# Products of a zero tile on TensorE before the first transpositions, the first block's q products and the first projection

## The chip, the cores and the metric

The kernel runs on one core of a Trainium2 chip. The metric is the device time in microseconds (us). Three runs of the kernel before took 623.01, 628.4 and 629.44 us, so the median is 628.4 us.

## The reference

An attention layer with a memory term feeds a gated feed-forward layer.

```
scores = q @ k.T / 8, causal;  a = softmax(scores);  local = a @ v
q_p    = elu(q) + 1
mem    = (q_p @ M_prev) / (q_p @ z_prev + 1e-6)
x      = sigmoid(beta) * mem + (1 - sigmoid(beta)) * local     # 4 x 8 heads x 576 rows x 64
x      = x / rms(x) * rms_g                                    # 2304 x 512
out    = (silu(x @ w_gate) * (x @ w_val)) @ w_out              # 512 -> 1536 -> 512
```

The weights of the second layer come as 64-bit floats and are converted on the chip.

## The kernel before

The 2304 rows are 18 blocks of 128 rows, and two blocks make a chunk of 256 rows for the feed-forward layer. Blocks 0 and 1 are the first 128 rows of two batches. They, and two more, are computed in 32-bit floats; the others with pairs of 16-bit floats.

The start goes like this. `prep_qk32` (line 549) transposes k and q of a block on TensorE, four 128x128 tiles each, through `transposed` (line 528). The result stands in a PSUM tile of the tag `gv`, which has two buffers, and ScalarE or VectorE copies it out (lines 533 and 535). `prep_phi32` (line 557) does the same with elu(q)+1. `over_partitions` (line 255) finds a maximum over the partitions with two small products (lines 258 and 261). `u_scores` multiplies q by k (line 597), VectorE adds the mask and takes the row maximum (line 614), ScalarE takes the exponentials (line 666), TensorE transposes them (line 531) and `pv32` multiplies by v (line 811). `mem32` makes the memory term (lines 788 and 792). VectorE scales the local part (line 827), GpSimd adds it to the memory part (line 829). `x_norm` (line 898) squares and sums a block on ScalarE (line 391) and takes the root on GpSimd (line 904). `x_float` (line 908) then makes a diagonal matrix of the factor on VectorE (line 915), multiplies by it on TensorE (line 918), and VectorE writes the transposed block (line 919).

When blocks 0 and 1 are there, `m_proj` (line 1092) starts the projections of chunk 0 (line 1102, 32-bit) into a `gv` tile, and `m_act` takes them on ScalarE (line 1126) and VectorE (lines 1127 and 1130). From chunk 1 on the projections are 16-bit products (line 1109). `f64_to_f32` (line 1011) converts the 64-bit weights with two instructions on ScalarE (lines 1016 and 1020) and one on VectorE (line 1026), for each piece of 128 x 512; the pieces w0 to w23 come by DMA from SyncE's queue (line 978).

The order of the work on each engine is written out by hand in `ISSUE` (line 72): a letter for each kind of instruction, a number for how many of them, and `~n` for the one that stands n places further on in that kind. `T` is a transposition, `Z` one of the two small products, `S` a score product, `u` the memory term, `h` a product with v, `R` a product with the diagonal matrix, `G` a projection. Every engine works through its string in order, and `keep` (line 184) gives the instructions of a function their letter. TensorE's string begins `T8ZZ~1T8ZT4`, and around the first norm it has `s2R8G4G4~4`.

`mask` (line 291) is a 128 x 512 tile in 16-bit floats: VectorE sets it to zero (line 292), and GpSimd writes a triangle into its last 128 columns (line 293).

Of the kernel before, what the change touches and what calls it, by code (L numbers as in the profile page):

```python
# [70 lines left out]

ISSUE = {
    "PE": (
        "T8ZZ~1T8ZT4SS~1S~2S~3Zu4T4S5S~1S~2S~3T4S4u2Tu2Th4T4u4~4T2hTh3T2u4Th8ss~3ss~2ss~1s2R8G4G4~4GG~3GZG~2G3Z~1GZT4ZT4"
        "s4T4s4S8G6u4G2u4G8s~4ss~3ss~2sT4s~1s~5s2s~3ss~2ss~1s2~5s4s~1s2T4G6g9ZT4g20Zg3G2h4G5ZG2sGs~3ss~2sT4s~1ss3~1sZs3~1"
        "ss~1ss~3ss~2ss~1ss~1s4s4~4T4u4G8g6h4s8g22ZSS~1S~2S~3g16~4Zg4S4TG8u4T3Zg16DD~1D~2h4Z2D2T4DG6ZG2Dh4G8D2G8D9G32D4S"
        "S~7G16S14G3M9GMGMGMGMGM3G8S8G10S8G6D2SG24S7ZG24S5P12S3ZP12G22S16G14M8G4P12G8P12G12DD~2G11D2SD2GS~5DD~2D4G13DMP3M"
        "PSMPSS~3MPSS~2MPSS~1MPS2MPSMP15D6D~2G14D3S6DG9DD~2G5SGSGSGSGSGSGD2P24D3D~2GS6D4G13DD~2M8D4G4SGDD~2SGSGSGSGSG8D4"
        "G3MDD~2GMGMGMGMGMGD4GMGP25MPGPG3SGSGSGS3DD~2S3D4P9S3DD~2S4G24D4S4~2G6SGSG5P9G12S2D6G2P9G3SGSGSGSGSGSG14D6G5MGMGM"
        "GMGMP18GMGMGMG5SGSGSGSGSGSG2D6G5SGSGSGSGSGSP9G7SPGSPGSPGSPGSPGSPGPGP2D6G5MGMGMGMGMGMGMGMGP8GPG3SGSGSGSGSGSG2D6G5"  # L80
        "SGSGSGSGSGSG7P9G7D3SDSDSDGSGSGSP9GSGSG12SGSGSGSGSGSGSGSD6G5SGSGSGSGSP18GSGSGSG12D4MDMDMGMGMGP9MGMGMG12SGSGSGSGSG"
        "SGSGSD6G2P5GPGPGPSGPSGPSGPSGPSGSGSGSG5SGPSGPSGPSGPSGPSGPSGPSP5D6G9PGMPGMPGMPGMPGMPGMPGMPGMPGPGPGPGSGSGSGS5D6G9SG"
        "SGP10SGPSGPSGSGSGSG8D6GSGSP12GSGSGSGSGSGSG13SGP12SGSGS5D6G5SGSGSGSGSGSP12GSGSG12P12D6G5MGMGMGMGMGMGMGMG5SGSGSGSG"
        "SGSGSGSD6G5SGSP9GPSGPSGPSGSGSGSG5PGPGPGPGPGPGPGP5D3SDSDSDSGSGSGSGSGPGMPGMPGMPGMPGMPGMPGMPGMPGPGPGPGSGSGSGSGSGSGS"
        "GSD3PDPDPDGPGPGPGPGPSGPSGPSGPSGPSGSGSGSG5PGPGPGPGPGPGPGP5D4SDSDSGSGSGSGSGSPGSPGSPGSPGSPGSPGSPGSPGSPGPGPGPG3S2G5"
        "D3PDPDPDGPGPGS16PGPGPGPGPGPGPG8PGPGPGPGPGPGPS2GP4YPD4MDMDMGMGMGMGMGMS16GMGMGMGMGMGMGMGMG11D6G2S2G9S8G13D6S6PSPS"
        "P5S2P26GPGPGPGPGPGPGPGPGPGPGPGP2S8GPGPGPGPGPGPGPS8GPGPGPGPGP2S2PD6GPGPGPGPGPGPGPGPS16GPGPGPGPGPGPGPGPGPGPGPGPGP"
        "S2GPGPGP2S8P5~5PP~4PP~3PP~2DPP~1S8P~1PDPDPDPDPDPGPGPGS2PGPGPGPGPGPGPGPGPGPGPGPGPG6SGSGSGS5DSDSDS2DSDSDSM16S2GS"
        "G23D3S8D3G2P20P~10PP~9PP~8PP~7PP~6PP~5PP~4PP~3PP~2PP~1P11GPGPGPSGPSGPSGPSGPSGPSGPSGPSG5PGPGPGPGPGPGPGP5DPDPDPDPD"
        "PDPGPGPGPGPGPSGPSGPSGPSGPSGPSGPSGPSG5PGPGPGPGPGPGPGP5DPDPDPDPDPDPGPGPGPGPGPGPGPGPGPGPGPGPG5SGSGSGSGSGSGSGSD6G12"  # L90
        "M8G5MGMGMGMGMGMGMGMD6G9P24G15D5P12DG4SS~5G13PGPGPGPGPGPGPGP5D6G21S10G3D6G14S6M8S6G10D3MDMDMDMGMGMGMGMGS12G19D5P9"
        "S6DGP9G8SGSGSGSGSGSG8SGSGS6D6G13P9G6S2P9S6G5D6G14P18G3MGMGMGMGMYGMGMGMD3GS8D3G4S2P9S6G12SGSGSGSGSGSGSP9GSD6G17SG"
        "SGSGSGSGSGSGSD6S8G12M6P24M2G9P12G3D6G5SGSGSGSGSGSP12GSGSG12D6P12G24D6G13P12G11P12D6G17S2S2~6G7D4S12D2G2P12G7M8G3"
        "S16G12D6GM4GMGMSGMGMS3G14S4~2GS4G4D6P12D2D2~1S2P12S4D2S6G34MGMGMGMGMGMGMGMP12G7D6G6P12G18D3SDSDSDSGSGSP9G3PGPGPG"
        "PGPGPGPGPGPG4SGSGSGSGSGSG2D4MDMDM6P5G10PGPGPGPG4SGSGSGSGSGSG2D4PDPDPGPGPGPGPGPGPG11SGSGSGSGSGSG2D4PDPDPGPGPGPGPG"
        "PSGPSGSGSGSGSGSGSG5PGPGPGPGPGPGPGP2D4SDSDSGSGSGSGSGSPGPGPGPGPGPGPGPGPG11D3SDSDSDGSGSGSGSGSPGPGPGPGPGPGPGPGPG11D4"
        "MDMDMGMGMGMGMGMG12SGSGSGSGSGSGSGSD6G10P12G7SGSGSGSGSGSGSGSD3PDPDPDPGPGPGPGPGPGPGPGPGSGSGSGSGSGSGSGSG5MGMGMGM5D6G"
        "PGPGPGPGPGPGPGPGPGSPGSPGSPGSGSGSGSGSG4PGPGPGP5DPDPDPDPD2G9SGSGSGSGSGSGSGSG5PGPGPGP5DPDPDP2D2SDS2GSGSGSGSGSPGPGSP"
        "GSPGSPGSPGSPGSPGSPGSPGPGPG3S2G5D4PDPDPGPGPGPGS16PGPGPGPGPGPG8PGPGPGPGPGPGPS2GP3S8P2D6G5MGMGMS10GMGMGMGMGMG11M8G"
        "S11DSDSDSDSDSDG10P8S2P5GPGPGPGPGPGPGPP~10GPP~9GPP~8GPP~7GPP~6GPS8P~5GPS8P~4GPP~3PP~2PP~1P3DPDPDPDPDPDPGPGPGS2PGP"  # L100
        "GS8PGP~7PGP~6PGP~5PGP~4PGP~3PGS8P~2PGP~1PGPGPGPS2GPGPGPGPGP2GPGPGPGP3S8P2DPDPDPP~3S8PDP~2PDP~1PDPGPGPS2GPGPGPGPG"
        "PGPGPGPGPGPGPGPGPGPGS11PSGPSGPSGPSGPSGPGPGP3D6G4S2G20D2M16D4G24D6P15P7~15PP~14PP~13PP~12PP~11PP~10PP~9PP~8PP~7"
        "P15~22P15~37P52G24D6G24D8D2~1D2G48D6G24D6G24D6G24D6G24D6G24D6G24D6G24D6G24D6G24D6G24D8D2~1D4D2~1D2"
    ),
    "Activation": (
        "IfT2ITfT2IU2E4TU2E12N2fU9tU5tU4AU2ATU2oToTfE4AE4U2ATU2TU6AU4ATU4x2AU2xU2xU2E4xU2cU2xNU2AE4cxXU2U2~2cU2xAU2xU~1Ux"
# [1434 lines left out]
```

## Time and profile before

| | |
|---|---|
| median of three runs | 628.4 us |
| profiled execution | 622.36 us, with a span of 620.6 us |
| TensorE busy | 598.5 us, 96% of the span |
| weight loads on TensorE | 474.6 us, 76% |
| VectorE busy | 451.1 us, 73% |
| ScalarE busy | 396.8 us, 64% |
| GpSimd busy | 136.6 us, 22% |
| DMA | 87.57 MB |

The span goes from the first to the last instruction. PE is TensorE, DVE VectorE, ACT ScalarE, POOL GpSimd, SP SyncE. Busy time of PE is the union of its matmuls, and a matmul that runs at half the clock is busy for longer, so a busy PE may still be a slow one. [...]

### The profile page before, as it was taken

What the parts mean: (1) busy time and instruction counts of PE and PEld (TensorE: products, weight loads), DVE (VectorE), ACT (ScalarE), POOL (GpSimd) and SP (SyncE); (2) the same over time, 40 slices, a digit from 0 to 9 for tenths busy, and PEclk for the clock granted to TensorE, in tenths of its full rate; (3) what the DMA queues carried; (4) which work ended last, traced back from release to release, by engine and by line L of the source; (5) the groups of instructions that cost most, each with busy time, mean ns of one, the idle gap of its engine ahead of it and who ended that gap; (6) DMA issues with size and microseconds to landing.
All of it is one profiled execution on the core that took longest, in us unless ns stands there. A gap on an engine that the chain in (4) does not pass through costs nothing. (4 is left out here: it accounts for less than half of the span.)

```text
span 620.6 us, 15845 instructions
## 1 busy us (share of the span) xinstructions
PE 598.5 (96%) x6092; PEld 474.6 (76%) x6092; DVE 451.1 (73%) x1319; ACT 396.8 (64%) x856; POOL 136.6 (22%) x221
## 2 busy tenths in 40 slices
PE   5979999999999999999999999999999999999996
PEld 4868887677876878788888778778787888887774
DVE  3767688999999687776997777797886757853221
ACT  4587677999887667676466766875775644433221
POOL 2240001124323222121213221132221221112111
PEclk9989999999999999999999999999999999999999
DMA  7997336479868796887489379559995543520001
GB/s 264 361 335 295 103 124 202 135 172 229 149 107 164 149 178 116 176 162 125 71 146 167 80 154 188 106 109 161 164 158 108 86 91 72 94 54 18 35 1 35
DMA packets 183787, 87.57 MB, mean 141 GB/s; under 512 B 165792, under 2 KB 165792, under 8 KB 183712
## 3 DMA queue, kind: packets, MB, share of 16 engines
q1 hardware_dynamic: 180640, 81.82, 62.0%
q10 hardware_dynamic: 3072, 4.74, 2.3%
q8 instruction: 48, 0.79, 0.5%
q14 instruction: 27, 0.22, 0.1%
HBM read 37.77 MB, written 4.72 MB: 68 GB/s over the span
## 5 line engine op out<-in xcount | busy, mean ns | idle before, releaser
L1109 PE MATMUL gv<-xT,wgv 128*128 128x256 f16 x2304 | 312.6, 273 | 0.7 <-DMA xT<-x 0.5
L1109 PEld LDWEIGHTS <-wgv 128*128 128x128 f16 x2304 | 220.0, 98 | 38.9 <-issue 1.5
L1148 POOL TENSOR_TENSOR h<-th,h 128x256 f16<-128x256 f32 x88 | 65.8, 748 | 291.1 <-ACT h L1147 283.8
L674 ACT ACTIVATE S<-S,nm 128x256 f32<-128x256 f32 (+3 forms) x112 | 70.8, 639 | 41.0 <-DVE nm L614 28.4
L1127 DVE SCALAR_TENSOR_TENSOR th<-th,gv 128x256 f32<-128x256 f32 x96 | 39.9, 415 | 62.0 <-ACT th L1126 61.7
L608 PE MATMUL sc<-kT,qT 128*128 128x128 f16 x576 | 79.3, 220 | 0.8 <-DVE nm L614 0.5
L693 DVE SCALAR_TENSOR_TENSOR P<-S,P 128x512 f16<-128x512 f32 (+2 forms) x96 | 67.4, 703 | 17.4 <-ACT P L190 16.8
L1126 ACT ACTIVATE th<-gv,wt 128x256 f32<-128x256 f32 x96 | 44.5, 463 | 54.3 <-PE gv L1109 50.1
L614 DVE CUSTOM_DVE_ANT_0 S<-sc,mask,qsc 128x256 f32<-128x256 f32 (+2 forms) x96 | 57.4, 610 | 17.2 <-PE sc L608 16.7
L1184 PE MATMUL out<-wo,h 128*128 128x512 f16 x176 | 66.8, 380 | 0.0
L1183 PE MATMUL out<-wo,h 128*128 128x512 f16 x176 | 66.3, 379 | 0.0
L1185 PE MATMUL out<-wo,h 128*128 128x512 f16 x176 | 66.1, 379 | 0.0
L190 ACT ACTIVATE P<-S 128x512 f16<-128x512 f32 (+2 forms) x96 | 58.0, 605 | 12.7 <-DMA PT<-P 10.7
L1147 ACT CAST h<-th 128x256 f16<-128x256 f32 x88 | 35.1, 399 | 46.5 <-DVE th L1130 39.0
L608 PEld LDWEIGHTS <-qT 128*128 128x128 f16 x576 | 48.3, 98 | 7.3 <-issue 1.8
L1102 PE MATMUL gv<-xT,wgv 128*128 128x256 f32 x192 | 46.9, 395 | 0.8 <-DVE xT L919 0.8
L1130 DVE SCALAR_TENSOR_TENSOR th<-th,wt,gv 128x256 f32<-128x256 f32 x96 | 45.8, 477 | 1.8
L1102 PEld LDWEIGHTS gv<-xT,wgv 128*128 128x128 f32 x192 | 36.6, 197 | 7.7 <-issue 1.9
L731 PE MATMUL loc<-v,PT 128*128 128x65 f16 x288 | 40.9, 193 | 1.0 <-DMA PT<-P 1.0
L733 PE MATMUL loc<-v,PT 128*128 128x65 f16 x288 | 41.2, 193 | 0.0
L732 PE MATMUL loc<-v,PT 128*128 128x64 f16 x288 | 40.6, 194 | 0.0
L1185 PEld LDWEIGHTS <-h 128*128 128x128 f16 x176 | 17.1, 98 | 19.5
(231 smaller groups left out, 1133.5 us busy)
## 6 DMA issues: line engine op xcount, KB each, us to landing
kv<-in_qkv_dram SPq DMA_DIRECT2D x40, 256.0 KB, 3.6
q<-in_qkv_dram SPq DMA_DIRECT2D x18, 256.0 KB, 3.5
wo<-in_moe_w_out_dram SPq DMA_DIRECT2D x8, 512.0 KB, 3.9
out_dram<-res ACTq DMA_DIRECT2D x16, 256.0 KB, 3.2
wgv<-in_moe_w_val_dram SPq DMA_DIRECT2D x7, 512.0 KB, 7.7
wo<-in_moe_w_gate_dram SPq DMA_DIRECT2D x7, 512.0 KB, 9.1
qT<-qT SPq DMA_DIRECT2D x28, 128.0 KB, 3.5
wgv<-in_moe_w_gate_dram SPq DMA_DIRECT2D x5, 512.0 KB, 6.2
```

The source lines that it names most:

```text
L190: got = fn(*p, **k)
L608: nc.tensor.matmul(t[:, g * w + j * P : g * w + (j + 1) * P], qT[n][:, t2, h, :], kT[blk_of[(b, j)]][:, h, :], start=(t2 == 0), stop=(t2 = ...
L614: nc.vector.tensor_tensor_reduce(out=s[:, g * w : (g + 1) * w], in0=t[:, g * w : (g + 1) * w], in1=mask[:, m0 : m0 + w], scale=qsc[n][:, 5 ...
L674: nc.scalar.activation(v_, v_, AF.Exp, bias=nm[:, g : g + 1], scale=-1.0)
L693: m = nc.vector.scalar_tensor_tensor(out=p16[:, w : 2 * w], in0=s[:, :w], scalar=PSCALE, in1=p16[:, :w], op0=ALU.mult, op1=ALU.subtract)
L1102: nc.tensor.matmul(o, wgv[:, 1 + p, o0 : o0 + P], xT[0][:, cc, :], start=(cc == 0), stop=(cc == NC - 1))
L1109: nc.tensor.matmul(o, lhs, xT[c][:, rhs, :], start=(cnt == 0), stop=(cnt == 3 * NC - 1))
L1130: nc.vector.scalar_tensor_tensor(out=th, in0=th, scalar=sc_h, in1=gvp[F][:, 1, :], op0=ALU.mult, op1=ALU.mult)
L1148: nc.gpsimd.tensor_tensor(h16[:, 1], th, h16[:, 0], ALU.subtract)
L1183: nc.tensor.matmul(o, hh, whi, start=(f == 0), stop=False)
L1184: nc.tensor.matmul(o, hh, wlo, start=False, stop=False)
L1185: nc.tensor.matmul(o, hl, whi, start=False, stop=(f == NF - 1))
```

## The change

A new helper, `idle`, multiplies a zero tile (the first 128 columns of `mask`) by another (the next 256 columns). The product goes to a tile that the next real product overwrites. It is called in three places, and the new letter `*` puts the products in TensorE's string: 20 ahead of the first transposition, 8 ahead of the transposition of block 0's elu(q)+1, and 25 for the first projection's tile, of which 20 stand between the four `R` of block 0 and the four of block 1, and 5 between these and the first projection. Nothing else moves: without the new letters all strings are the same.

```diff
-        "T8ZZ~1T8ZT4SS~1S~2S~3Zu4T4S5S~1S~2S~3T4S4u2Tu2Th4T4u4~4T2hTh3T2u4Th8ss~3ss~2ss~1s2R8G4G4~4GG~3GZG~2G3Z~1GZT4ZT4"
+        "*20T8*8ZZ~1T8ZT4SS~1S~2S~3Zu4T4S5S~1S~2S~3T4S4u2Tu2Th4T4u4~4T2hTh3T2u4Th8ss~3ss~2ss~1s2R4*20R4*5G4G4~4GG~3GZG~2"
+    @keep("*")
+    def idle(t, count):
+        for _ in range(count):
+            nc.tensor.matmul(t, mask[:, :P], mask[:, P : 3 * P], start=True, stop=True)
+
     @keep("T")
-    def transposed(dst, src, on_act):
+    def transposed(dst, src, on_act, wait=0):
         t = ps.tile([P, NC, P], F32, tag="gv", name="tp")
+        idle(t[:, :2], wait)
...
-        transposed(k32[n], src32(n, 0), T32[0] == "a")
+        transposed(k32[n], src32(n, 0), T32[0] == "a", 20 if n == 0 else 0)
...
-        transposed(q32[n][:, 1], qst.pop(n), T32[2] == "a")
+        transposed(q32[n][:, 1], qst.pop(n), T32[2] == "a", 8 if n == 0 else 0)
...
         if m == 0:
             gvp[F] = ps.tile([P, 2, 2 * P], F32, tag="gv", name=f"gv{F}")
+            if F == 0:
+                idle(gvp[F][:, 0], 25)
```

## Rows read from the trace of the kernel before

**Rows 1.** The page: granted TensorE clock in 40 slices of 15.5 us, tenths

```profile
PEclk9989999999999999999999999999999999999999
```

**Rows 2.** Busy time by stretch: PE, PEld, DVE, ACT, POOL, granted clock, DMA

```profile
9.00:21.00 12.00, 11.98 (x55) 10.13 (x56) 4.42 (x26) 6.96 (x18) 2.28 (x5) 1.00 0.98 375
21.00:29.00 8.00, 8.00 (x72) 7.54 (x71) 7.38 (x44) 4.74 (x25) 1.45 (x2) 1.00 1.04 351
60.00:620.00 560.00, 551.04 (x5807) 434.13 (x5805) 415.12 (x1172) 357.54 (x750) 122.77 (x187) 1.00 0.62 122
```

**Rows 3.** TensorE in order, 6 to 29 us: start, duration, [idle before, releaser]

```profile
6.18 1.09 PE L531 MATMUL tp<-ident,kv 128*128 128x128 f32 x4 [6.18 <-DMA kv<-in_qkv_dram]
...
9.02 0.59 PE L258 MATMUL allp<-ident,zq 128*1 128x128 f32 x2 [0.89 <-ACT junk L391]
...
15.93 2.08 PE L788 MATMUL mem<-Mpair,q 128*128 128x128 f32 x8
...
21.24 0.66 PE L531 MATMUL tp<-ident,S 128*128 128x128 f32 x4
...
27.56 1.06 PE L788 MATMUL mem<-Mpair,q 128*128 128x128 f32 x8
```

**Rows 4.** Busy time by stretch around the first norm, columns as in Rows 2

```profile
30.80:34.20 3.40, 2.04 (x22) 1.84 (x21) 1.85 (x4) 1.47 (x4) 1.82 (x4) 1.00 1.02 355
34.20:37.60 3.40, 1.16 (x8) 0.97 (x8) 3.12 (x7) 3.40 (x7) 3.16 (x5) 1.00 0.69 233
37.60:41.00 3.40, 3.37 (x8) 2.75 (x9) 2.01 (x3) 3.40 (x8) 1.59 (x3) 0.50 0.98 309
```

**Rows 5.** TensorE in order, 31 to 84 us

```profile
31.73 1.11 PE L918 MATMUL xtp<-diag,t 128*128 128x128 f32 x8
35.69 1.16 PE L918 MATMUL xtp<-diag,t 128*128 128x128 f32 x8 [2.85 <-DVE ph L515]
37.63 6.68 PE L1102 MATMUL gv<-xT,wgv 128*128 128x256 f32 x22 [0.78 <-DVE xT L919]
...
79.73 3.62 PE L1102 MATMUL gv<-xT,wgv 128*128 128x256 f32 x16
```

**Rows 6.** Chain of waits: start, duration, 16-bit products of 128x256 in a row

```profile
609.19 2.62 PE gv L1109 x24
```

**Rows 7.** VectorE and GpSimd in order, 1 to 3 us

```profile
1.06 0.27 DVE L292 MEMSET mask<- 128x256 uint32 x1
...
2.21 0.29 POOL L293 TENSOR_SCALAR_AFFINE_SELECT mask<-mask 128x128 bf16<-128x128 bf16 x1
```

**Rows 8.** ScalarE in order, 7 to 47 us

```profile
7.31 0.58 ACT L533 COPY k<-tp 128x512 f32<-128x512 f32 x1 [1.35 <-PE tp L531]
...
8.64 0.23 ACT L391 ACTIVATE junk<-zz 128x32 bf16<-128x32 f32 x1
...
14.40 0.65 ACT L1016 ACTIVATE wgv<-wgv 128x512 f32<-128x512 f32 x1
...
15.87 0.40 ACT L666 ACTIVATE S<-S,nm 128x128 f32<-128x128 f32 x1 [0.25 <-DVE nm L614]
...
19.38 0.67 ACT L1016 ACTIVATE wgv<-wgv 128x512 f32<-128x512 f32 x1
...
21.14 0.40 ACT L666 ACTIVATE S<-S,nm 128x128 f32<-128x128 f32 x1 [0.54 <-DVE nm L614]
...
46.15 0.38 ACT L1126 ACTIVATE h32e<-gv 128x256 f32<-128x256 f32 x1 [0.85 <-PE gv L1102]
```

**Rows 9.** VectorE in order, 15 to 32 us

```profile
15.53 0.29 DVE L614 CUSTOM_DVE_ANT_0 S<-sc,mask 128x128 f32<-128x128 f32 x1 [0.89 <-PE sc L597]
...
20.81 0.29 DVE L614 CUSTOM_DVE_ANT_0 S<-sc,mask 128x128 f32<-128x128 f32 x1 [3.38 <-PE sc L597]
...
31.47 0.42 DVE L827 TENSOR_TENSOR t<-loc,den 128x256 f32<-128x256 f32 x1
```

**Rows 10.** DMA issues between 8.5 and 9.0 us: KB, us from issue to landing

```profile
wgv<-in_moe_w_gate_dram SPq DMA_DIRECT2D x1, 512.0 KB, 4.8
```

More of the change, by code (lines that the diff above doesn't have):

```diff
@@ L73 @@
     "PE": (
-        "T8ZZ~1T8ZT4SS~1S~2S~3Zu4T4S5S~1S~2S~3T4S4u2Tu2Th4T4u4~4T2hTh3T2u4Th8ss~3ss~2ss~1s2R8G4G4~4GG~3GZG~2G3Z~1GZT4ZT4"
-        "s4T4s4S8G6u4G2u4G8s~4ss~3ss~2sT4s~1s~5s2s~3ss~2ss~1s2~5s4s~1s2T4G6g9ZT4g20Zg3G2h4G5ZG2sGs~3ss~2sT4s~1ss3~1sZs3~1"
-        "ss~1ss~3ss~2ss~1ss~1s4s4~4T4u4G8g6h4s8g22ZSS~1S~2S~3g16~4Zg4S4TG8u4T3Zg16DD~1D~2h4Z2D2T4DG6ZG2Dh4G8D2G8D9G32D4S"
-        "S~7G16S14G3M9GMGMGMGMGM3G8S8G10S8G6D2SG24S7ZG24S5P12S3ZP12G22S16G14M8G4P12G8P12G12DD~2G11D2SD2GS~5DD~2D4G13DMP3M"
@@ L78 @@
[L78 to L102, printed above, removed]
@@ L103 @@
-        "P15~22P15~37P52G24D6G24D8D2~1D2G48D6G24D6G24D6G24D6G24D6G24D6G24D6G24D6G24D6G24D6G24D8D2~1D4D2~1D2"
+        "*20T8*8ZZ~1T8ZT4SS~1S~2S~3Zu4T4S5S~1S~2S~3T4S4u2Tu2Th4T4u4~4T2hTh3T2u4Th8ss~3ss~2ss~1s2R4*20R4*5G4G4~4GG~3GZG~2"
+        "G3Z~1GZT4ZT4s4T4s4S8G6u4G2u4G8s~4ss~3ss~2sT4s~1s~5s2s~3ss~2ss~1s2~5s4s~1s2T4G6g9ZT4g20Zg3G2h4G5ZG2sGs~3ss~2sT4"
+        "s~1ss3~1sZs3~1ss~1ss~3ss~2ss~1ss~1s4s4~4T4u4G8g6h4s8g22ZSS~1S~2S~3g16~4Zg4S4TG8u4T3Zg16DD~1D~2h4Z2D2T4DG6ZG2Dh4"
+        "G8D2G8D9G32D4SS~7G16S14G3M9GMGMGMGMGM3G8S8G10S8G6D2SG24S7ZG24S5P12S3ZP12G22S16G14M8G4P12G8P12G12DD~2G11D2SD2GS~5"
@@ new lines @@
+        "DD~2D4G13DMP3MPSMPSS~3MPSS~2MPSS~1MPS2MPSMP15D6D~2G14D3S6DG9DD~2G5SGSGSGSGSGSGD2P24D3D~2GS6D4G13DD~2M8D4G4SGDD~2"
+        "SGSGSGSGSG8D4G3MDD~2GMGMGMGMGMGD4GMGP25MPGPG3SGSGSGS3DD~2S3D4P9S3DD~2S4G24D4S4~2G6SGSG5P9G12S2D6G2P9G3SGSGSGSGSG"
+        "SG14D6G5MGMGMGMGMP18GMGMGMG5SGSGSGSGSGSG2D6G5SGSGSGSGSGSP9G7SPGSPGSPGSPGSPGSPGPGP2D6G5MGMGMGMGMGMGMGMGP8GPG3SGSG"
+        "SGSGSGSG2D6G5SGSGSGSGSGSG7P9G7D3SDSDSDGSGSGSP9GSGSG12SGSGSGSGSGSGSGSD6G5SGSGSGSGSP18GSGSGSG12D4MDMDMGMGMGP9MGMGM"
+        "G12SGSGSGSGSGSGSGSD6G2P5GPGPGPSGPSGPSGPSGPSGSGSGSG5SGPSGPSGPSGPSGPSGPSGPSP5D6G9PGMPGMPGMPGMPGMPGMPGMPGMPGPGPGPGS"
@@ new lines @@
+        "GSGSGS5D6G9SGSGP10SGPSGPSGSGSGSG8D6GSGSP12GSGSGSGSGSGSG13SGP12SGSGS5D6G5SGSGSGSGSGSP12GSGSG12P12D6G5MGMGMGMGMGMG"
+        "MGMG5SGSGSGSGSGSGSGSD6G5SGSP9GPSGPSGPSGSGSGSG5PGPGPGPGPGPGPGP5D3SDSDSDSGSGSGSGSGPGMPGMPGMPGMPGMPGMPGMPGMPGPGPGPG"
+        "SGSGSGSGSGSGSGSD3PDPDPDGPGPGPGPGPSGPSGPSGPSGPSGSGSGSG5PGPGPGPGPGPGPGP5D4SDSDSGSGSGSGSGSPGSPGSPGSPGSPGSPGSPGSPGSP"
+        "GPGPGPG3S2G5D3PDPDPDGPGPGS16PGPGPGPGPGPGPG8PGPGPGPGPGPGPS2GP4YPD4MDMDMGMGMGMGMGMS16GMGMGMGMGMGMGMGMG11D6G2S2G9S8"
+        "G13D6S6PSPSP5S2P26GPGPGPGPGPGPGPGPGPGPGPGP2S8GPGPGPGPGPGPGPS8GPGPGPGPGP2S2PD6GPGPGPGPGPGPGPGPS16GPGPGPGPGPGPGPGP"
@@ new lines @@
+        "GPGPGPGPGPS2GPGPGP2S8P5~5PP~4PP~3PP~2DPP~1S8P~1PDPDPDPDPDPGPGPGS2PGPGPGPGPGPGPGPGPGPGPGPGPG6SGSGSGS5DSDSDS2DSDSD"
+        "SM16S2GSG23D3S8D3G2P20P~10PP~9PP~8PP~7PP~6PP~5PP~4PP~3PP~2PP~1P11GPGPGPSGPSGPSGPSGPSGPSGPSGPSG5PGPGPGPGPGPGPGP5D"
+        "PDPDPDPDPDPGPGPGPGPGPSGPSGPSGPSGPSGPSGPSGPSG5PGPGPGPGPGPGPGP5DPDPDPDPDPDPGPGPGPGPGPGPGPGPGPGPGPGPG5SGSGSGSGSGSGS"
+        "GSD6G12M8G5MGMGMGMGMGMGMGMD6G9P24G15D5P12DG4SS~5G13PGPGPGPGPGPGPGP5D6G21S10G3D6G14S6M8S6G10D3MDMDMDMGMGMGMGMGS12"
+        "G19D5P9S6DGP9G8SGSGSGSGSGSG8SGSGS6D6G13P9G6S2P9S6G5D6G14P18G3MGMGMGMGMYGMGMGMD3GS8D3G4S2P9S6G12SGSGSGSGSGSGSP9GS"
@@ new lines @@
+        "D6G17SGSGSGSGSGSGSGSD6S8G12M6P24M2G9P12G3D6G5SGSGSGSGSGSP12GSGSG12D6P12G24D6G13P12G11P12D6G17S2S2~6G7D4S12D2G2"
+        "P12G7M8G3S16G12D6GM4GMGMSGMGMS3G14S4~2GS4G4D6P12D2D2~1S2P12S4D2S6G34MGMGMGMGMGMGMGMP12G7D6G6P12G18D3SDSDSDSGSGS"
+        "P9G3PGPGPGPGPGPGPGPGPG4SGSGSGSGSGSG2D4MDMDM6P5G10PGPGPGPG4SGSGSGSGSGSG2D4PDPDPGPGPGPGPGPGPG11SGSGSGSGSGSG2D4PDPD"
+        "PGPGPGPGPGPSGPSGSGSGSGSGSGSG5PGPGPGPGPGPGPGP2D4SDSDSGSGSGSGSGSPGPGPGPGPGPGPGPGPG11D3SDSDSDGSGSGSGSGSPGPGPGPGPGPG"
+        "PGPGPG11D4MDMDMGMGMGMGMGMG12SGSGSGSGSGSGSGSD6G10P12G7SGSGSGSGSGSGSGSD3PDPDPDPGPGPGPGPGPGPGPGPGSGSGSGSGSGSGSGSG5M"
@@ new lines @@
+        "GMGMGM5D6GPGPGPGPGPGPGPGPGPGSPGSPGSPGSGSGSGSGSG4PGPGPGP5DPDPDPDPD2G9SGSGSGSGSGSGSGSG5PGPGPGP5DPDPDP2D2SDS2GSGSGS"
+        "GSGSPGPGSPGSPGSPGSPGSPGSPGSPGSPGPGPG3S2G5D4PDPDPGPGPGPGS16PGPGPGPGPGPG8PGPGPGPGPGPGPS2GP3S8P2D6G5MGMGMS10GMGMGMG"
+        "MGMG11M8GS11DSDSDSDSDSDG10P8S2P5GPGPGPGPGPGPGPP~10GPP~9GPP~8GPP~7GPP~6GPS8P~5GPS8P~4GPP~3PP~2PP~1P3DPDPDPDPDPDPG"
+        "PGPGS2PGPGS8PGP~7PGP~6PGP~5PGP~4PGP~3PGS8P~2PGP~1PGPGPGPS2GPGPGPGPGP2GPGPGPGP3S8P2DPDPDPP~3S8PDP~2PDP~1PDPGPGPS2"
+        "GPGPGPGPGPGPGPGPGPGPGPGPGPGPGS11PSGPSGPSGPSGPSGPGPGP3D6G4S2G20D2M16D4G24D6P15P7~15PP~14PP~13PP~12PP~11PP~10PP~9P"
@@ L104 @@
+        "P~8PP~7P15~22P15~37P52G24D6G24D8D2~1D2G48D6G24D6G24D6G24D6G24D6G24D6G24D6G24D6G24D6G24D6G24D8D2~1D4D2~1D2"
     ),
```

## The prediction

> **What bounds the kernel now.** I began with the page and its strip of the granted clock: it shows a dip in the third slice alone, so nearly the whole span seems to run at full clock [rows 1]. Busy time by stretch came next. From 60 us to 620 us TensorE is busy 551.0 of 560 us; it is the bound there, and whatever it reaches earlier at 60 us it keeps to the end [rows 2]. So the change is priced in the first 60 us alone.
>
> There the strip misleads. TensorE in order shows the same instruction at two prices: four transpositions take 1.09 us at 6.18 and 0.66 us at 21.24, and the eight products of the memory term take 2.08 us at 15.93 and 1.06 us at 27.56 [rows 3]. [...] So the row's 1.00 for 9 to 21 us [rows 2] is no grant that was recorded: TensorE runs at half clock there, with 11.98 of 12 us busy. The second half-clock stretch is recorded: 0.50 from 37.6 to 41 us, after a stretch in which the engine had only 1.16 of 3.40 us of work, and it rose again when the projections had run without a pause [rows 4]. The first 22 instructions of the projection take 6.68 us there, while 16 take 3.62 us at full clock [rows 5].
>
> **The change part by part.** It removes and moves nothing; it adds 53 products to TensorE's queue, and no DMA or other engine's instruction. At full clock 24 products of this shape take 2.62 us, 0.109 us each [rows 6]; at half clock I put 0.218 (an estimate from the same row, by the factor of rows 3).
>
> *The 20 at the start.* They need the zero part of the tile, which is there at 1.06 + 0.27 = 1.33 us, or, if the wait takes in the whole tile, at 2.21 + 0.29 = 2.50 us [rows 7]. At half clock they take 4.4 us and end at 5.7 or 6.9 us. The transpositions behind them wait for a DMA until 6.18 us [rows 3], so the cost is 0 to 0.7 us. If the clock has risen by then, the first eight transpositions take 1.3 us in place of 2.15, which pays that back. I take 0.
>
> *The 8.* Their tile has the buffer of the first transpositions, free when ScalarE has copied it at 7.31 + 0.58 = 7.89 us [rows 8]. At full clock they end at 7.89 + 0.87 = 8.76 us, before the small product behind them can start at 9.02 us; the ScalarE sum that it waits for covers them [rows 3, 8]. At half clock they end at 9.63 us, 0.6 late. I take 0.1.
>
> *What full clock is worth from 9 to 21 us.* TensorE's 12.0 us become 6.0 [rows 2], so the second batch of scores, for which VectorE waits 3.38 us until 20.81 [rows 9], could be there at about 15.4 us: 5.4 earlier. ScalarE gains less. Its first weight conversion (14.40) can't start before its piece has landed, issued at 8.6 us or so and 4.8 us under way [rows 10]: 13.4 us. Conversion 1.1, four exponentials at 0.39 each 1.6, a copy 0.5, conversion 1.1: the second batch of exponentials starts at 17.7 in place of 21.14 [rows 8], 3.5 earlier. Which of the two sets the end of the block? Twelve exponentials at 0.39 us (4.7) end at 22.4; a transposition 0.66, a copy 0.6 and a product of about 1.0 (as the memory term's, rows 3) put the last scaling of the local part at 25 us or later. VectorE is busy 7.38 of 8 us between 21 and 29 [rows 2], so its queue moves as a whole and reaches that scaling 5.4 earlier than 31.47 [rows 9], at 26.1. VectorE comes last. The ends are 3.5 and 5.4; I take **5.0**, nearest to VectorE's row, with 0.4 for its waits on ScalarE.
>
> *The 25 around the norm.* Twenty take 2.2 us in a pause of 2.85 us, five take 0.55 us in one of 0.78 us [rows 5]: the chain ScalarE, GpSimd, VectorE of the second block's norm covers them. The engine then works some 3.9 of 5 us where it had sat. From 30.8 to 34.2 us it worked 2.04 of 3.40 us and the next stretch still began at full clock [rows 4], so I expect no fall. The 22 instructions then take 22 x 3.62/16 = 5.0 us in place of 6.68, 1.7 less [rows 5]. Late next is ScalarE: it has no pause from 34.2 to 41 us [rows 4] and waits only 0.85 us for the projection at 46.15 [rows 8]. Between 0.85 and 1.7 I take **0.9**, as TensorE soon needs the buffers that this ScalarE instruction helps to free.
>
> The sum, against the profiled execution: 622.4 - 5.0 - 0.9 + 0.1 = 616.6 us. That execution lies 6.0 us under the median of 628.4, and two of three runs lie 6 to 7 above it. Which part of them is longer no row shows. A half-clock stretch that lasts longer in some executions would be taken away with the rest; anything else would stay. I add 2.4 of the 6.0: **619 us**.
>
> **The rivals.** *The clock falls back, or never rises, at the start.* Much of what follows the 20 products is transpositions and products of one row or column. For it: TensorE had no pause from 9.0 us on, full of such work, and was still at half clock past 17 us, whereas the projections brought the clock up within the 3.4 us of their stretch [rows 2 to 4]. Against it: once up, the clock stayed up through 21 to 34 us, where transpositions and small products are mixed in. The 5.0 are then lost and the 8 cost 0.6; the norm's 0.9 stay: 622.4 - 0.9 + 0.6 = 622.1 us, and 624.5 with the same 2.4. [...] The transpositions at 21.24 us, which ran at full clock behind other products, show at least that they can be served at it [rows 3].
>
> *TensorE is faster but the others are not.* ScalarE's two conversions hold the block as far as its row says: 3.5 in place of 5.0, thus 618.1, and 620.5 with the 2.4. For it stands the landing at 13.4 us, which no TensorE clock moves; against it the order worked out above.
>
> *Slower.* If the clock stands at half when the norm of block 0 ends, the 20 products take 4.4 us in a pause of 2.85, and the second block's eight products stand behind them on TensorE: 1.5 late. These eight take 0.9 more, and the five behind them 1.1 us in 0.78: 0.3. The projection, and ScalarE's first activation behind it, start 2.7 late. With the early 0.7 and 0.6 that is 622.4 + 4.0 = 626.4, 628.8 with the 2.4, and up to 632.4 with the whole 6.0. It decides from the point at which the stretch before the norm is too thin to keep the clock. Against it: that stretch is at full clock now [rows 4], and in front of it the zero products can only add work.
>
> That the products do nothing at all, because a zero tile doesn't move the clock, gives the first rival's time without the 0.9: about 623, and 625.5.
>
> **How the numbers follow.** The forecast has 0.60 (its own range 613.5 to 622), the first rival with its zero-tile variant 0.22, ScalarE's bound 0.12, the slower one 0.06. The range of 613.5 to 626.5 us takes in the forecast with the whole 1.7 of the norm and without the 2.4, ScalarE's bound, and most of the first rival; it leaves out the slower one and executions that carry the whole 6.0. One per cent, about what a measurement can tell from no change here, is 6.3 us, so faster by that means under 622.1. The forecast falls there in three of four cases (0.45), ScalarE's bound in two of three (0.08), the first rival in few (0.02): 0.55. Slower by one per cent means over 634.7, which needs the slow rival and more: 0.04. The rest is 0.41.
>
> **What would show it.** In the profile after, four transpositions at 6 to 10 us should take 0.66 us, the memory term at about 12.6 us 1.06; VectorE's second batch of score reductions should start near 15.4 us, the second batch of exponentials near 17.7, the last scaling near 26.3 and the projections near 32.6 us with 0.226 us for each instruction. A memory term that still takes 2.08 us shows the first rival. VectorE with pauses before the last scaling shows ScalarE's bound. Zero products at 0.218 us between the two norms show the slow one. The prediction is wrong too if TensorE is early at 60 us but has more than 9 us of pauses behind it.

## The result, and the profile after

The changed kernel takes 627.73 us, the median of 20 runs (624.11 to 629.91), against 623.16 us for the kernel before, the median of 20 runs beside them (618.87 to 631.59). The ratio is 1.0102, with an interval of 1.0086 to 1.0117, where I had forecast 619.0 us and faster. The ratio compares the change with the eleven runs of the kernel before from 618.87 to 623.18 us and leaves out the nine from 628.40 to 631.59; with all twenty the medians' ratio is 627.73/623.16 = 1.0073 and that of the means 627.60/625.11 = 1.004, still slower.

Two things happened. TensorE's clock rose early, as forecast, at 6.2 us, but fell again at 19.9 us, and by 60 us nothing was left of the gain. Then, from 60 us to the end, where the change has no instruction, another 5.8 us were lost.

The profiled execution takes 628.82 us (span 627.1). The page, engines (share of the span, instructions) and the strip of the granted clock, beside [rows 1]. That strip dips once, to 8 in its third slice; this one dips to 6 in its second slice and to 8 in its third:

```profile
PE 608.4 (97%) x6145; PEld 481.6 (77%) x6145; DVE 451.0 (72%) x1319; ACT 396.8 (63%) x856; POOL 135.9 (22%) x221
...
PEclk9689999999999999999999999999999999999999
```

TensorE in order, kernel after (start, duration, [idle before, releaser]; it answers to [rows 3] and [rows 5]):

```profile
1.39 4.45 PE L530 MATMUL tp<-mask 128*128 128x256 bf16 x20 [1.39 <-DVE mhalf L290]
5.92 0.77 PE L538 MATMUL tp<-ident,kv 128*128 128x128 f32 x4
...
12.16 1.16 PE L795 MATMUL mem<-Mpair,q 128*128 128x128 f32 x8
15.56 1.48 PE L538 MATMUL tp<-ident,S 128*128 128x128 f32 x4 [0.17 <-ACT S L673]
17.54 1.16 PE L604 MATMUL sc<-k,q 64*128 64x128 f32 x8 [0.50 <-DVE nm L621]
18.63 0.61 PE L799 MATMUL zn<-zpair,q 128*128 128x2 f32 x4
26.25 1.91 PE L795 MATMUL mem<-Mpair,q 128*128 128x128 f32 x8
33.18 2.02 PE L925 MATMUL xtp<-diag,t 128*128 128x128 f32 x8
34.99 3.31 PE L530 MATMUL gv<-mask 128*128 128x256 bf16 x20
38.13 1.06 PE L925 MATMUL xtp<-diag,t 128*128 128x128 f32 x8
39.97 5.01 PE L1111 MATMUL gv<-xT,wgv 128*128 128x256 f32 x22 [0.24 <-DVE xT L926]
58.30 3.70 PE L1111 MATMUL gv<-xT,wgv 128*128 128x256 f32 x16
```

The same work has two prices within one trace. The memory term of block 0 takes 1.16 us at 12.16, where it took 2.08 before [rows 3]; that of block 1 takes 1.91 us at 26.25, where it took 1.06. Full clock and half clock have changed places. The 20 products between the norms take 3.31 us, as the clock rises only while they run, at 36.94 us, and the first projections then take 5.01 us instead of 6.68 [rows 5], but start 2.3 us later.

Busy time by stretch, kernel after (time and count of PE, PEld, DVE, ACT, POOL, then granted clock, DMA share, GB/s; the columns of [rows 2]):

```profile
15.50:19.80 4.30, 3.57 (x23) 2.69 (x24) 3.73 (x25) 4.30 (x19) 0.00 (x0) 1.00 1.02 410
19.80:23.30 3.50, 3.50 (x20) 3.50 (x19) 2.61 (x15) 3.05 (x16) 0.00 (x0) 0.51 1.03 404
...
37.00:40.00 3.00, 2.76 (x26) 2.32 (x24) 3.00 (x6) 3.00 (x6) 2.64 (x4) 1.00 0.95 308
290.00:450.00 160.00, 153.55 (x1809) 121.98 (x1807) 127.93 (x367) 106.04 (x220) 38.51 (x60) 1.00 0.71 127
```

The clock is at full from 6.22 to 19.87 us, at half behind it, and at full again from 36.94 us, while the 20 products run. The stretch before the fall has 0.7 us of pauses in 4.3, and part of its busy time is products of 2 columns and transpositions that each wait for an exponential: four take 1.48 us at 15.56 and took 0.66 [rows 3].

ScalarE in order, kernel after (beside [rows 8]):

```profile
13.90 0.66 ACT L1023 ACTIVATE wgv<-wgv 128x512 f32<-128x512 f32 x1 [1.36 <-DMA wgv<-in_moe_w_gate_dram]
18.14 0.38 ACT L673 ACTIVATE S<-S,nm 128x128 f32<-128x128 f32 x1
```

VectorE in order, kernel after (beside [rows 9]):

```profile
15.84 0.28 DVE L621 CUSTOM_DVE_ANT_0 S<-sc,mask 128x128 f32<-128x128 f32 x1
32.56 0.42 DVE L834 TENSOR_TENSOR t<-loc,den 128x256 f32<-128x256 f32 x1 [1.87 <-PE loc L818]
```

The second batch of score reductions starts at 15.84 instead of 20.81 us, 5.0 us early. The last scaling of the local part starts at 32.56 instead of 31.47, 1.1 us late, after 1.87 us of waiting for TensorE.

From 290 to 450 us TensorE is busy for 153.55 of 160 us. The same stretch of the kernel before:

```profile
290.00:450.00 160.00, 157.73 (x1875) 127.05 (x1873) 129.54 (x376) 106.53 (x221) 38.53 (x60) 1.00 0.74 132
```

That is 4.2 us more of pauses in one stretch far behind the change. What TensorE waits for from 60 to 620 us, kernel after (us in total, times, longest):

```profile
PE loc L738 <- DMA PT<-P: 2.5, 3, 1.9
```

The same view, kernel before:

```profile
PE loc L731 <- DMA PT<-P: 1.0, 2, 0.6
```

All waits that the view lists add up to 9.0 us after and 4.7 us before. At the head of the list of after stand products that wait for a DMA transposition.

### The profile page after: what moved, and what is told of

The parts are those of the page before. It is cut to its first block, busy times and chain, and to the rows that moved or that the text cites. A ratio compares the mean times of both kernels' runs of the same rounds, so it can differ in the third digit from the quotient of the medians.

```text
span 627.1 us, 15950 instructions
## 1 busy us (share of the span) xinstructions
PE 608.4 (97%) x6145; PEld 481.6 (77%) x6145; DVE 451.0 (72%) x1319; ACT 396.8 (63%) x856; POOL 135.9 (22%) x221
## 5 line engine op out<-in xcount | busy, mean ns | idle before, releaser
L1111 PE MATMUL gv<-xT,wgv 128*128 128x256 f32 x192 | 45.2, 384 | 0.2 <-DVE xT L926 0.2
L1111 PEld LDWEIGHTS gv<-xT,wgv 128*128 128x128 f32 x192 | 35.3, 190 | 6.9 <-issue 1.9
L1194 PEld LDWEIGHTS <-h 128*128 128x128 f16 x176 | 17.2, 98 | 19.5
```

The costliest lines, as they stand in the source:

```text
L1111: nc.tensor.matmul(o, wgv[:, 1 + p, o0 : o0 + P], xT[0][:, cc, :], start=(cc == 0), stop=(cc == NC - 1))
L1194: nc.tensor.matmul(o, hl, whi, start=False, stop=(f == NF - 1))
```

## The experiments

To compare the traces I use one ruler: the start of the same two TensorE instructions in each, the 16 projections that stand at 57.62 us in the trace of before, and the 48 projections at 567.41 us. "At 60 us" and "at the end" below are how much later than that they start. The traces come from several chips.

The expectations name theories by letters, and each states its own. In short: A puts the difference down to TensorE's clock in the first 60 us; B to a part behind 60 us that varies by itself and has nothing to do with the kernel; C, formed after the first four runs, says that some executions of the kernel before are long because the clock rises late in them; D, formed at the same time, says that the added TensorE instructions shift the fetches of TensorE's own program, which then fall on the DMA transpositions.

**The kernel before, once more.** No edit; timed beside the next three.

> The kernel before, unchanged, for the granted clock of each of its runs and a second trace. Theory A (the clock in the first 45 us decides the time): runs near 629 us have a lower mean clock than runs near 621, by 0.007 or more (about 8 us more at half clock), and the trace of a slow one stands several us behind the first trace at 60 us. Theory B (the time is decided after 60 us, by waits for DMA and VectorE that come out one way or another): runs near 629 and near 621 have the same clock within 0.003, and two traces that stand within 1 us of each other at 60 us end up to 8 us apart.

Median 625.91 us of 12 runs, ratio 0.9995 (0.9967 to 1.0022). Its profiled execution was an odd one of 3508.07 us and shows nothing. The others lie in two groups, six from 619.92 to 622.25 and five from 629.56 to 631.05 us, with the same mean granted clock in both (0.995 at 621.54 and at 630.48 us). Theory A's lower mean clock isn't there. So the mean clock doesn't tell the groups apart; the traces below do.

**Only the 25 around the norm.**

```diff
-        "*20T8*8ZZ~1T8ZT4SS...
+        "T8ZZ~1T8ZT4SS...
-        transposed(k32[n], src32(n, 0), T32[0] == "a", 20 if n == 0 else 0)
+        transposed(k32[n], src32(n, 0), T32[0] == "a", 0)
-        transposed(q32[n][:, 1], qst.pop(n), T32[2] == "a", 8 if n == 0 else 0)
+        transposed(q32[n][:, 1], qst.pop(n), T32[2] == "a", 0)
```

> The 25 products around the norm alone, without the 20 and the 8 at the start. Theory A: the start is as in the kernel before, the rise near 20.5 us included; the 25 are hidden in the pauses of 2.85 and 0.78 us; the half-clock stretch at 37.6 us is gone and the 22 instructions of the first projection take 5.0 us in place of 6.68; at 60 us 1 to 1.7 us ahead of the kernel before, ratio 0.997. Theory B: no more than that at 60 us either, but the end anywhere from -2 to +7 us. Rival: the 20 products come to stand ahead of the second norm's products and delay them, 0 or +1 us at 60 us.

627.81 us (6 runs, 622.85 to 631.88), ratio 1.0101 (1.0032 to 1.0171). Three of the six lie from 622.85 to 624.80 us and three from 630.81 to 631.88, so here too there are two groups; the trace is of the run of 624.80. In it the first 22 projections start at 35.17 us and take 5.02; at 60 us it is 2.41 us early, at the end 2.40 late. The gain in the first 60 us is more than the 1 to 1.7 expected, but not the norm's: the clock rises at 12.05 us and not near 20.5, and the last scaling stands at 28.99 us, 2.48 early, ahead of the 25. What they save in the projections is gone again by 60 us, behind another half-clock stretch from 46.19 to 49.60 us. And 4.8 us are lost behind 60 us.

The clock of this kernel also falls, with no zero product at the start. Its busy time by stretch:

```profile
12.10:22.20 10.10, 10.10 (x85) 9.19 (x86) 9.15 (x60) 9.21 (x37) 0.72 (x1) 1.00 1.01 396
22.30:25.70 3.40, 3.40 (x19) 3.40 (x18) 1.93 (x8) 0.88 (x5) 1.45 (x2) 0.50 1.06 321
```

It falls at 22.29 us, after 10.10 us without a pause, and is back at 25.71. The work of the last 5 us of this, from 17.2 us on, the kernel before does at 21.2 to 26.4 us, also without a pause (8.00 of 8 us busy from 21 us on [rows 2]), and keeps its clock.

**Only the 28 at the start.**

```diff
-...ss~1s2R4*20R4*5G4G4~4...
+...ss~1s2R8G4G4~4...
-                idle(gvp[F][:, 0], 25)
+                idle(gvp[F][:, 0], 0)
```

> The 20 and the 8 products at the start alone, without the 25 around the norm. Theory A: full clock from 6 us, 4 to 5 us ahead at 18 us, a fall near 20 us as in the changed kernel, then half clock through the norms and into the projections until about 41 us: the second norm's products are not held up by the 20 any more (1 us less), but 22 instructions of the projection take 6.7 us or more; at 60 us 0.5 to 2.5 us behind the kernel before, and 0 to 1.5 us behind the changed kernel. If the fall comes from the 25 or is a matter of chance, it is ahead by 4 us or more.

628.25 us (6 runs, 627.35 to 628.75), ratio 1.0100 (1.0072 to 1.0129). TensorE in order, kernel with the 28 alone:

```profile
37.13 2.07 PE L925 MATMUL xtp<-diag,t 128*128 128x128 f32 x8 [1.95 <-DVE diag L922]
39.98 6.99 PE L1111 MATMUL gv<-xT,wgv 128*128 128x256 f32 x22 [0.78 <-DVE xT L926]
```

Its busy time by stretch:

```profile
20.10:44.00 23.90, 20.58 (x91) 19.01 (x91) 14.11 (x38) 13.78 (x40) 8.46 (x14) 0.50 0.99 323
```

The clock falls at the same place and stays at 0.50 for 23.9 us, into the projections. At 60 us it is 2.67 us late, a little more than expected, and the whole change in its first trace 0.68: the two stand 2.0 us apart there. With the 25 the clock is back at 36.94 us, without them at 44.02. In that trace of the whole change the 20 also hold up the second norm's products by 1.0 us (38.13 against 37.13).

**The whole change, with the sparse stretch filled.** 22 further products stand ahead of three of the transpositions in the part where the clock fell.

```diff
+FILL = {(0, 4): 6, (1, 0): 8, (1, 4): 8}
-...S~3T4S4u2Tu2Th4T4u4~4T2hTh3...
+...S~3T4*6S4u2Tu2Th4*8T4u4~4T2h*8Th3...
-            transposed(Pt[(n, h0)], Ssb.pop((n, h0)), T32[3 + h0 // 2 % 2] == "a")
+            transposed(Pt[(n, h0)], Ssb.pop((n, h0)), T32[3 + h0 // 2 % 2] == "a", FILL.get((n, h0), 0))
```

> The changed kernel with 22 more zero products inside the first two blocks: 6 ahead of the second half of block 1's scores, 8 after the first products with v, 8 before the last transposition of exponentials. Theory A: these keep the clock up from 6 us to the projections; no half clock between 20 and 37 us; the first projection starts at 33 to 34 us in place of 39.97, and at 60 us the kernel stands 4 to 6 us ahead of the kernel before. Rival: TensorE is already full in that stretch, the 22 cost 2.4 us and more, and the clock falls all the same because the stretch waits for VectorE and ScalarE: 2 to 3 us behind the changed kernel at 60 us.

620.85 us (12 runs, 618.22 to 626.29), ratio 0.9983 (0.9946 to 1.0020). Busy time by stretch, kernel with the filled stretch:

```profile
15.50:19.80 4.30, 4.05 (x28) 2.94 (x28) 3.75 (x25) 4.30 (x18) 0.00 (x0) 1.00 1.03 416
19.80:23.30 3.50, 3.50 (x35) 3.42 (x35) 2.43 (x14) 2.94 (x16) 0.00 (x0) 1.00 1.03 400
23.30:30.10 6.80, 6.04 (x59) 5.82 (x58) 4.36 (x13) 0.72 (x2) 3.39 (x6) 1.00 1.04 320
```

TensorE in order, the same kernel:

```profile
17.05 0.81 PE L531 MATMUL tp<-mask 128*128 128x256 bf16 x6
30.33 2.35 PE L531 MATMUL gv<-mask 128*128 128x256 bf16 x20
35.30 5.01 PE L1112 MATMUL gv<-xT,wgv 128*128 128x256 f32 x22 [0.26 <-DVE xT L927]
```

VectorE in order, the same kernel:

```profile
29.12 0.42 DVE L835 TENSOR_TENSOR t<-loc,den 128x256 f32<-128x256 f32 x1 [0.24 <-PE loc L819]
```

The clock stays up in this trace, and the last scaling comes at 29.12 us, 2.35 earlier than before [rows 9] and 3.4 earlier than in the change. The 20 products between the norms take 2.35 us and the projections start at 35.30 us, 2.33 early. At 60 us the kernel is 3.15 us early, less than the 4 to 6 expected; 0.8 of that is the norm's products', against 0.9 forecast. I put it down to the price of the filling that only 2.35 of the 5.0 is left: its 22 products take some 0.81 + 1.04 + 1.04 = 2.9 us on a TensorE that has hardly a pause there. This run shows the fall of the clock to be what took the early gain. At the end it is 0.95 us early: 2.2 us are lost behind 60 us. Nine of the twelve runs lie from 618.22 to 621.40 us at a mean clock of 0.995 to 1.000, three from 624.92 to 626.29 at 0.987 to 0.991, so the filling doesn't seem to hold the clock every time.

**Traces of the kernel before, three, and of the change, one more.** No edits.

> The kernel before, unchanged, for another trace. It comes out near 621 us or near 629.5 us. Theory C (the two groups are made at the start): TensorE is at half clock longer in an execution near 629.5, until the first projections at 37 us or later, and it is 6 us or more behind at 60 us; in one near 621 the clock rises between 12 and 21 us. Theory B (made after 60 us): the traces stand within 2 us of each other at 60 us, and part between 140 and 450 us.

> As the run before it: the kernel before, unchanged. Theory C: half clock up to the first projections goes with 629.5 us, a rise between 12 and 21 us with 621. Theory B: no such tie, within 2 us at 60 us.

> As the two before it: the kernel before, unchanged. Theory C: half clock up to the first projections goes with 629.5 us, a rise between 12 and 21 us with 621. Theory B: no such tie, within 2 us at 60 us.

> The changed kernel, unchanged, for a second trace. Theory A: the clock rises near 6 us, falls between 16 and 24 us and stays at half until the 20 products between the norms, in this execution too; at 60 us it stands within 2 us of its first trace. If the fall was a matter of chance, the clock stays up and the kernel is 3 us or more ahead of its first trace at 60 us.

629.26, 632.25, 621.41 and, for the change, 627.47 us. TensorE in order, first of the three:

```profile
21.61 1.11 PE L531 MATMUL tp<-ident,S 128*128 128x128 f32 x4
33.34 1.91 PE L788 MATMUL mem<-Mpair,q 128*128 128x128 f32 x8
35.24 1.00 PE L811 MATMUL loc<-kv,PT 128*128 128x64 f32 x8
```

Its busy time by stretch:

```profile
21.00:35.00 14.00, 14.00 (x67) 13.22 (x66) 7.51 (x41) 5.42 (x26) 1.45 (x2) 1.00 1.03 327
```

In the two long executions the transpositions at 21.6 and 21.4 us and the second memory term still run at half clock; the clock rises only at 35.2 us. They are 7.7 and 7.6 us late at 60 us. The row's 1.00 is again no grant that was recorded: four transpositions take 1.11 us under it, against 0.66 at 21.24 us in [rows 3]. The short one has the clock up from 19.4 us and is 0.97 us early. So theory C holds in these three: what parts the long executions of the kernel before from the short ones is when its clock rises. The change's second trace has the clock at half from 19.11 to 29.35 us, is 0.31 us early at 60 us, and loses 5.4 behind it, as the first lost 5.8. The fall is there again, as expected. That the clock would stay at half until the 20 products was wrong: it is back ahead of them, and they take 2.35 us at 33.15.

**How many instructions are added, alone.** Small zero products (32 weight columns, 16 or 64 moving columns; each counted as a weight load and a product, two instructions: the page of after has 6145 of both, that of before 6092) in place of the wide ones. First 53 of them, so the change's 106 instructions, ahead of the first transposition of the kernel before, and nothing else:

```diff
-        "T8ZZ~1T8Z...
+        "*53T8ZZ~1T8Z...
+    def small(t, count):
+        for _ in range(count):
+            nc.tensor.matmul(t[:32, 0, :16], mask[:, :32], mask[:, P : P + 16], start=True, stop=True)
```

> The kernel before with 53 small products (32 columns of weights, 16 moving columns) ahead of the first transposition and nothing else: 106 instructions more on TensorE, as many as in the changed kernel, in a wait for a DMA. Theory D (the time lost after 60 us comes from where the fetches of TensorE's instructions fall among the DMA transpositions): between 100 us and the end the trace loses 4 to 6 us against the first trace of the kernel before, as both traces of the changed kernel do. Theory E (it is what the early start leaves behind, through the order of buffers and loads): no loss, within 2 us. The start itself is as before, or the clock rises earlier.

The same with 128 of them, 256 instructions:

```diff
-        "*53T8ZZ~1T8Z...
+        "*128T8ZZ~1T8Z...
```

> The kernel before with 128 small products at the same place: 256 instructions more, one whole piece of 16 KB of TensorE's program. Theory D: the fetches fall where they do in the kernel before, and from 100 us to the end the trace stays within 2 us of it. Theory E: as the run before it. If it is the number as such, more is lost than with 106.

Then the change, with 95 small products (64 moving columns) in place of its first 20, which makes its 53 products 128:

```diff
-        "*20T8*8ZZ~1T8Z...
+        "*95T8*8ZZ~1T8Z...
```

> The changed kernel with 95 small products (32 columns of weights, 64 moving columns) in place of its first 20, so that 256 instructions are added in all and not 106. Theory D: from 100 us to the end within 2 us of the kernel before, in place of 5.1 to 5.8 behind, so 623 to 625 us if the start is as in the changed kernel. Theory E: 627 to 629 us, with 4 us or more lost after 100 us. The small products may not raise the clock at the start; then the start is as in the kernel before.

And the kernel with the filled stretch, with 73 in place of the 20, 128 products again:

```diff
-        "*20T8*8ZZ~1T8Z...
+        "*73T8*8ZZ~1T8Z...
```

> The changed kernel with the 22 products inside the first two blocks, and 73 small ones in place of the first 20: 256 instructions added in all. If the clock is up by 12 us it keeps full clock to the projections and stands 2.5 to 3.5 us ahead of the kernel before at 60 us. Theory D: it keeps that to the end, 618 to 620 us. Theory E: no different from the 620.85 us of the kernel with the 22 products and the 20 whole ones, 1 to 3 us lost after 100 us.

They took 634.11 us (4 runs, ratio 1.0152, 1.0071 to 1.0233), 623.29 (10 runs, 0.9995, 0.9940 to 1.0050), 621.61 (10 runs, 0.9933, 0.9889 to 0.9977) and 622.14 us (10 runs, 1.0015, 0.9959 to 1.0072). All traces on the ruler, in us:

| kernel | instructions added | at 60 us | at the end | lost between |
|---|---|---|---|---|
| before, three more traces | 0 | +7.69, +7.60, -0.97 | +6.81, +9.80, -1.03 | -0.9, 2.2, -0.1 |
| the 25 alone | 50 | -2.41 | +2.40 | 4.8 |
| the 28 alone | 56 | +2.67 | +6.41 | 3.7 |
| before, 53 small | 106 | +7.53 | +11.74 | 4.2 |
| the change, two traces | 106 | +0.68, -0.31 | +6.48, +5.11 | 5.8, 5.4 |
| the change, filled | 150 | -3.15 | -0.95 | 2.2 |
| before, 128 small | 256 | +7.18 | +8.09 | 0.9 |
| the change, 95 small | 256 | +0.28 | +0.85 | 0.6 |
| the filled one, 73 small | 256 | -3.08 | -3.05 | 0.0 |

The rows that carry the verdict are the 48 projections near the end in the chain of waits (start, duration, line, count). Kernel before, kernel after, before with 53 small products, before with 128, the change with 95, one row each:

```profile
567.41 5.24 PE gv L1109 x48
```

```profile
573.89 5.24 PE gv L1118 x48
```

```profile
579.15 5.24 PE gv L1124 x48
```

```profile
575.50 5.24 PE gv L1124 x48
```

```profile
568.26 5.24 PE gv L1124 x48
```

The 53 small products cost nothing where they stand. TensorE in order, that kernel:

```profile
1.39 1.58 PE L536 MATMUL tp<-mask 128*32 128x16 bf16 x53 [1.39 <-DVE mhalf L290]
5.84 1.09 PE L544 MATMUL tp<-ident,kv 128*128 128x128 f32 x4 [2.87 <-DMA kv<-in_qkv_dram]
```

They are done 2.87 us before their successor's data come, and don't bring the clock up. In both traces of the old kernel with small products the clock rises only at 35.0 and 34.5 us, so both are late at 60 us, to 0.35 us the same, and what comes behind it compares the two. There 106 instructions lose 4.2 us and 256 lose 0.9. The medians of the two don't compare: all four runs with 53 products (633.85 to 637.71 us) are long ones, but only three of the ten with 128 (629.10 to 630.55, the trace's 630.43 among them); the other seven take 620.45 to 623.73. Long against long, 634.11 stands against 630.43. The change with 95 small products has the same fall of the clock as the change (half from 18.29 to 28.53 us) and carries 75 products more, yet takes 621.61 us where the change, in another session, takes 627.73: by the table, 5.2 us of that lie behind 60 us.

Where the time is lost speaks for D too. Every trace has the same 6092 products in the same order once the zero ones are left out. By the starts of the same products, between those at 260 and 290 us of the kernel before the kernels with 50 and 56 added instructions lose 1.8 us each, although one is early and the other late. Between 290 and 320 us the three traces with 106 lose 1.7 to 1.8 each, the old kernel with its late clock like the change. None of the other three traces of the kernel before and none of the three with 256 loses 0.1 us in either. Theory E, which needs the early start, has no place for that.

Why 256? The DMA view of the changed kernel, a queue whose packets are marked as instructions (packets, MB, share of 16 engines):

```profile
q8 instruction: 48, 0.79, 0.5%
```

0.79 MB in 48 packets are 16 KB each. TensorE has 6145 products and 6145 weight loads by the page above, and 12290/48 = 256. The kernel before has 48 packets for 12184, and the kernels with 256 more have 49. In all thirteen traces TensorE starts 253 to 255 instructions on average from one packet to the next. So q8 brings TensorE's program, and one packet holds some 256 of its instructions, about 627.1/48 = 13 us of TensorE's work; 256 more leave every later packet where it was in the work, 106 more shift it by two fifths of a packet. The packets' starts show that shift: against the kernel before, a packet comes some 24 products earlier in the work with 50 or 56 instructions added, 46 to 48 earlier with 106, and where it was, to 2 products, with 256 (medians).

What a packet does to a transposition, in the DMA view of five microseconds ahead of the loss at 290 to 320 us, kernel before (packets, MB, share; for transpositions the median us to landing):

```profile
xT<-x SPq DMA_TRANSPOSE x1, 3.3
kT<-row SPq DMA_TRANSPOSE x1, 3.3
PT<-P SPq DMA_TRANSPOSE x1, 3.1
```

The same work in the kernel after:

```profile
q8 instruction: 1, 0.02, 1.2%
...
xT<-x SPq DMA_TRANSPOSE x1, 5.3
kT<-row SPq DMA_TRANSPOSE x1, 4.8
PT<-P SPq DMA_TRANSPOSE x1, 4.2
```

A packet of q8 has come in there that wasn't, and the three transpositions take 4.2 to 5.3 us in place of 3.1 to 3.3. Over all 158 transpositions of a trace, those during which such a packet is under way take 4.22 us on average (57 of them) and those with no instruction packet 3.23 (83) in the kernel before; in the kernel after 4.09 (63) and 3.21 (81). A transposition that takes long for another reason also has more time to meet a packet; counting only packets within 2.7 us of the issue the means are 4.09 and 3.42 us before, 4.02 and 3.37 after. So the price of a meeting is some 0.7 to 1 us in both; which transpositions meet one is not the same.

One transposition can be followed through all traces, the 102nd of the 158, for which TensorE waits. TensorE in order, the product behind it in the kernel after, in the kernel before with 53 small products, in the kernel before, and in that with 128:

```profile
404.83 0.20 PE L738 MATMUL loc<-v,PT 128*128 128x65 f16 x1 [1.89 <-DMA PT<-P]
```

```profile
410.03 0.20 PE L744 MATMUL loc<-v,PT 128*128 128x65 f16 x1 [1.53 <-DMA PT<-P]
```

```profile
398.55 0.20 PE L731 MATMUL loc<-v,PT 128*128 128x65 f16 x1 [0.33 <-DMA PT<-P]
```

```profile
406.52 0.20 PE L744 MATMUL loc<-v,PT 128*128 128x65 f16 x1 [0.22 <-DMA PT<-P]
```

In the three traces with 106 instructions and the one with 150 a packet starts 0.1 to 2.2 us behind its issue; it takes 5.2 to 5.5 us and TensorE waits 1.5 to 1.9. In the other nine no packet starts before 3.2 us; it takes 3.8 to 4.0 us.

## Why the prediction was wrong

**What held.** The clock rose early: at 6.2 us, behind the 20 products. The memory term took 1.16 us at 12.16 (forecast 1.06 at 12.6), the first conversion waited for its landing until 13.90 (13.4), the score reductions came at 15.84 (15.4) and the second exponentials at 18.14 (17.7). The norm's 25 were worth 0.8 us in the trace whose clock stays up (0.9), and the first 22 projections took 5.01 us (5.0).

**"Once up, the clock stayed up".** This step failed. I took the kernel before, where the clock stays up from 21 to 34 us, as proof that this kind of work keeps it. But there TensorE was late, and its work stood ready: 8.00 of 8 us busy [rows 2]. Brought forward by 5 us it runs ahead of the exponentials and waits for them, 3.57 of 4.30 us busy, and the clock falls at 19.9 us. The rest of the block runs at half clock: 5.0 us early at 15.84 becomes 1.1 late at 32.56. The kernel with the filled stretch, which differs by 22 products there, keeps the clock up, so the fall is what took the gain. What makes the clock fall is not shown. The waits can't be all of it: with the 25 alone it fell after 10.10 us without one, in work that the kernel before runs as densely and at full clock.

My first rival had the event and nearly the size. It put the change 0.3 us ahead of the profiled execution (622.1 against 622.4), where the traces stand at +0.68 and -0.31 at 60 us, the size in part by luck: the 8, which it had 0.6 late, ran at full clock, in 1.03 us at 7.36. I gave it 0.22. Its reason was the transpositions and the products of one row or column. But transpositions ran at full clock up to 19.87 us, four in 0.60 to 0.77 us where they didn't wait (1.09 at half clock [rows 3]), and with the stretch filled the clock stayed up over those behind it (four in 0.60 us at 21.71, against 1.06 at 21.23 in the change). Whether transpositions and narrow products hold the clock less well than others, no run here tells. Nor was "below nothing" in the term's bounds; it should have been, since the clock of the kernel before falls as well, to 0.50 at 37.6 us [rows 4].

The rival on the slower side was near in its place in the first trace: the 20 products did run into a lower clock, 3.31 us against my 2.2 at full and 4.4 at half, and delayed the second norm's products by 1.0 us. In the second trace they ran at full clock, in 2.35 us. I had its condition (a stretch before the norm too thin to keep the clock) but gave it 0.06, with the trace of before as its refutation. That trace couldn't refute it: the change makes the block a different one. By 60 us all this comes to +0.68 us in the first trace and -0.31 in the second, in place of -5.8.

**"Whatever it reaches earlier at 60 us it keeps to the end".** This step failed by 5.8 and 5.4 us in the two traces. I had priced 53 products as 53 products and "no DMA". They are 106 instructions, and TensorE's program itself comes by DMA, by the count above in 48 packets of 16 KB. Leaving out the clock, the same 106 instructions in the kernel before lose 4.2 us, and 256 lose 0.9. Three traces of one unchanged kernel differ by -0.9 to 2.2 us behind 60 us, so by its size alone a loss of 2.2 for 150 instructions isn't told from nothing, while 3.7 to 5.8 is.

**The base.** I summed against an execution of 622.36 us and added 2.4 for the gap to the median of 628.4. Three runs gave that median; the twenty beside the change, eleven short and nine long, have 623.16. By the three traces the gap is the late rise of the clock, at 35 us instead of 20.5 as in the execution that I summed against, worth 7.6 to 7.7 us at 60 us in part of the executions. In both traces of the change the clock is up by 6.2 us, and its 20 runs form one group. So the early products do take that part away, but what they leave, 627.7 us, lies far nearer to the long executions than to the short ones.

What stays open: why the clock of the kernel before rises at 35 us in some executions and at 19 in another, and at 12.05 us with the 25 alone, whose start is the same; why the clock falls after dense work in one kernel and not in another; why transpositions stretch by 1 to 2 us beside a packet that itself takes 1.12 us on average (48 packets, before and after alike); and how the losses of 2.2 us and less divide.

Of all kernels here, the change with 95 small products has the best ratio, 0.9933 (0.9889 to 0.9977), and the filled one the lowest median, 620.85 us, at 0.9983. What the first wins is the long executions: all ten of its runs lie from 618.25 to 623.25 us. The thirteen short runs of the kernel before beside it have a median of 620.81, 0.8 us under its 621.61, and its trace is 0.85 us late. Filled and padded together (the last kernel) the profiled execution took 619.3 us and kept all 3.1 us, but the median of 622.14 us misses the 618 to 620 expected; four runs of ten take 624.05 to 627.53 at a lower mean clock (0.987 to 0.990), as three of the filled kernel do.
